# Weights asked for in nine pieces instead of six, and a new order of the steps: a linear-attention layer and a token and channel mixer on one core

## The chip, the cores and the metric

The kernel runs on one core of a Trainium2 chip. The time is the device time of one execution in microseconds; before the change its median is 165.49 us over 3 runs (165.25 to 165.77).

## What is computed

The inputs r, k and v have 4 batches, 8 heads, 768 positions and 48 values per head. A linear attention with decay `w` and bonus `u` runs along the positions; its output x has, for each batch, 768 positions of 384 values. Behind it stands a mixer: a two-layer net along the positions, added to x, and a two-layer net along the 384 channels, added again.

```python
def _attn_ref(r, k, v, w, u):
    for t in range(S):
        cur = np.einsum('bhd,bhe->bhde', u[None] * kt, vt)
        y[:, :, t] = np.einsum('bhd,bhde->bhe', rt, state + cur)
        state = w[None, :, :, None] * state + np.einsum('bhd,bhe->bhde', kt, vt)

def _moe_ref(x, w_tok1, w_tok2, w_ch1, w_ch2):
    xt = x.transpose(0, 2, 1)
    h = np.maximum(xt @ w_tok1, 0.0) @ w_tok2
    u = x + h.transpose(0, 2, 1)
    h2 = np.maximum(u @ w_ch1, 0.0) @ w_ch2
    return (u + h2)
```

## The kernel before

**The work.** The positions are cut into chunks of 128, six to a batch, so there are 24 units (a batch and a chunk), counted from 0. For each unit `u` the names of the steps are: `kp` and `rp`, the products of k and r with powers of the decay (tiles `kpr` from `ld_k` and `ld_r`), on VectorE or GpSimd; `vb`, a cast of v on ScalarE; `trk` and `trr`, their transposes on TensorE (`tr_ps`) and `rkk`, `rkr` or `rk`, the copies out of PSUM in two halves or in one (tile `rk`); `at`, the scores (`at_ps`); `AT0` and `AT1`, the masked scores, one half of which may go by ScalarE (`raw`); `kv` and `S`, the state; `pr` and `pg`, the bonus; `yd`, `yS` and `y`, the output (`y_ps`); `x`, the sum, which is the mixer's input (`x_b`).

For each batch `b` the mixer has: `hid`, the first token product over its six chunks (`h_ps<-x_b,wtok`), `hr`, its relu (`h1r`); then `bk` and `us`, the second token product and its sum by chunk (`hT_ps`, `u_sb`), and `tu` and `uT`, the turn of each chunk (`t_ps`, `uT`); in batch 0's first half `ux` and `ub` make it turned at once (`at_ps` and `ut_ps`). Then come the channel nets for each half batch: 12 up steps `z` (`z_ps<-uT,wch`) of three matmuls, each read by a relu `zr`, and for each of three chunks the down step `h` (`h_ps<-wch,zr`) in four quarters of three matmuls. Quarters 0 and 1 of a down step read the first half of `w_ch2`, quarters 2 and 3 the second. `os` adds and `out` stores. So `z0_0_4` is batch 0, half 0, up step 4, and `h0_1_2` batch 0, chunk 1, quarter 2.

**The order.** `Step` (L35) and `Plan` (L45) are a list scheduler that runs while the kernel is built: `graph` (L168) adds the steps with the engines that may do them, what they wait for and a rank; `Plan.run` (L72) puts them in an order of time with the durations that are written beside them; in this order every engine's instructions are issued, and each engine works strictly in that order. `Plan.fill` (L129) puts idle matmuls into gaps of TensorE ahead of the first up step. All instructions are recorded by one helper at L512, so the profile shows that line for nearly all.

**The weights.** The four mixer weights are read from float32 in memory to bf16 tiles by DMAs that GpSimd issues, between its products: `wtok1` and `wtok2` whole, `wch1` (the up weight) and `wch2` (the down weight) in halves. Their place in GpSimd's order comes from `wafter` in `CFG`. The loads of k, r and v are issued by SyncE in the order of `transfers`; unit 6's k, and so all behind it, waits for unit 5's output (`hold`).

Of the kernel before, what the change touches and what calls it, by code (L numbers as in the profile page):

```python
# [24 lines left out]
C = S // T  # L25
G = C // 2
HP = H // 2
NJ = 12
# [6 lines left out]
class Step:  # L35
    def __init__(self, name, ways, after, take, give, rank, emit):
# [3 lines left out]
        self.engine = self.start = self.end = self.seen = self.sends = None  # L40
        for a in self.after:
            a.then.append(self)


class Plan:  # L45
# [26 lines left out]
    def run(self):  # L72
# [5 lines left out]
        while todo:  # L78
# [4 lines left out]
            while again:  # L83
                again = False
                for s in sorted(open_, key=lambda s: (s.rank, s.ready)):
                    if s.ready > now or (s.take and min(banks) > now):
                        continue
# [6 lines left out]
                    way = min(s.ways, key=lambda w: max(now, free.get(w[0], 0.0)) + w[2] + (w[4] if len(w) > 4 else 0.0))  # L94
# [73 lines left out]
def graph(do, cfg):  # L168
# [25 lines left out]
    loads, weights, fetched, gates, u_row = {}, {}, [], {}, None  # L194
    for n, (kind, i) in enumerate(cfg["transfers"]):
# [3 lines left out]
        elif kind != "w":  # L199
# [5 lines left out]
        else:  # L205
            weights[i] = n
    wx, wi = {}, {}

    def weight(i, after):
        wi[i] = s = p.add(f"i:w{i}", [("POOL", 0.9, cfg.get("wseen", 1.0), True)], after, rank=-50, emit=do("weight", i))  # L210
        took = cfg.get("wtime", (3.0, 2.6, 3.1, 7.7, 3.1) if 5 not in cfg["wafter"] else (3.0, 2.6, 3.1, 3.9, 3.1, 3.9))[i]
        wx[i] = p.transfer(f"x:w{i}", s, took, took + 1.0, -1.0)

    for i in cfg["wafter"]:
        weight(i, [])
    xs, S_prev, at_free, y_free, kv_read, yS_prev = {}, None, [], None, None, None
    kv_first, bank_read, scored = None, [], {}
    for u in range(NU):
# [22 lines left out]
        else:  # L241
# [12 lines left out]
            if u in by_pe:  # L254
                pr = p.add(f"pr{u}", [("DVE", cfg.get("prt", 0.5), 0.65)], [rk], rank=r - 0.3, emit=do("pr", u))
                reads.append(pr)
# [65 lines left out]
    for b in range(B):  # L322
# [5 lines left out]
        bank = [p.add(f"hid{b}_bank{i}", [("PE", 0.0, 0.0)], early + [wx[0]], take=True, rank=r) for i in range(2)]  # L328
        for c in range(C):
            h = p.add(f"hid{b}_{c}", [("PE", 2 * MM * f, 2 * MM * f + 0.13)], [xs[b * C + c], h] + bank, rank=r, emit=do("hid", b, c))  # L330
# [12 lines left out]
        for sg in range(2):  # L343
            if (b, sg) in direct:
                last = C * (b + 1) - 1
                for mm in range(3):
# [4 lines left out]
                    t = p.add(f"ub{n}", [("PE", 2 * MM + 0.01, 2 * MM + 0.14)], [t, wx[1]] + (hr if mm else first), rank=r - 0.2 + 0.01 * mm, emit=do("ub", b, sg, mm))  # L351
# [5 lines left out]
            for c in range(sg * G, sg * G + G):  # L357
                n = 3 if (b, c) in cfg.get("xpe", ()) else 2
                bk = p.add(f"bk{b}_{c}", [("PE", n * MM + 0.01 * (b > 0), n * MM + 0.13 + 0.01 * (b > 0))], hr + [wx[1]], take=True, rank=r + 0.01 * c, emit=do("bk", b, c))
# [636 lines left out]
```

## Time and profile before

| What | Value |
|---|---|
| median of 3 runs | 165.49 us |
| span of the profiled execution, first to last instruction | 166.5 us |
| TensorE busy | 156.8 us, 94% |
| VectorE, ScalarE, GpSimd busy | 106.8, 87.2, 65.3 us |
| mean granted clock of TensorE | 0.990 |
| chain that ended last | TensorE 79%, DMA 8%, GpSimd 5%, ScalarE 3% |

The profiled execution is one run of its own; of its time only the span is shown, which is 1.0 us over the median of the runs. Times within the trace are microseconds from the start of the span. In a timeline row stand start, length, engine, line, instruction, tiles written and read, count, and in brackets the idle time ahead of it and what ended that. Rows of the same kind are merged. A busy TensorE is not one at its peak, so its busy time is read along with the granted clock.

### The profile page before, as it was taken

The numbers are of one execution on the slowest core, as the hardware profiler recorded it, in microseconds if no ns is written. First come the engines' busy times: TensorE is split into PE (matmuls) and PEld (weight loads), VectorE is DVE, ScalarE is ACT, GpSimd is POOL, SyncE is SP. The second block draws the span as 40 slices with busy tenths as digits, with TensorE's granted clock in tenths as the row PEclk, the third lists the DMA queues.
The fourth block names the chain that finished last, engine by engine and source line by source line (L and its number), as shares of the span: only waits on it lengthen the run. The fifth ranks groups of instructions, "written<-read, shape, count | busy, mean of one in ns | idle before, by whom it ended". The sixth has DMA issues, their size and how long they took to land.

```text
span 166.5 us, 3791 instructions
## 1 busy us (share of the span) xinstructions
PE 156.8 (94%) x1462; PEld 100.6 (60%) x1464; DVE 106.8 (64%) x219; ACT 87.2 (52%) x182; POOL 65.3 (39%) x80
## 2 busy tenths in 40 slices
PE   6797999599999999999999999999999999999991
PEld 1377764356677666666666665666656655665671
DVE  5189996300459989899989889977885582021031
ACT  3996743279198636579804452069154502904900
POOL 7839970000009647386785857103840000000000
PEclk9999999789999999999999999999999999999999
DMA  5999999999699899999999994999990028012012
GB/s 100 215 213 210 159 187 176 188 184 168 131 208 287 158 192 216 217 230 182 198 192 169 230 158 106 188 235 222 171 240 6 4 50 218 16 51 94 0 47 94
DMA packets 97427, 26.26 MB, mean 158 GB/s; under 512 B 90753, under 2 KB 97410, under 8 KB 97410
## 3 DMA queue, kind: packets, MB, share of 16 engines
q1 hardware_dynamic: 93920, 22.88, 67.2%
q0 software_dynamic: 3488, 3.15, 12.3%
q8 instruction: 11, 0.18, 0.5%
q14 instruction: 6, 0.05, 0.1%
q10 hardware_dynamic: 2, 0.00, 0.0%
HBM read 20.65 MB, written 4.72 MB: 152 GB/s over the span
## 4 chain that ended last, share of the span: by engine, by line
PE 79%; DMA 8%; POOL 5%; ACT 3%; issue 2%; DVE 1%; SPq 1%; POOLq 0%
PE h_ps L512 31%; PE z_ps L512 29%; DMA wch<-in_moe_w_ch_dram 6%; PE y_ps L512 4%; PE at_ps L512 4%; PE hT_ps L512 3%; PE tr_ps L512 3%; POOL kpr L512 3%; PE kv_ps L512 2%; DMA ld_v<-in_v_dram 2%; PE t_ps L512 1%; ACT rk L512 1%; POOL wtok L512 1%; SPq L512 1%; POOL yd L512 0%
## 5 line engine op out<-in xcount | busy, mean ns | idle before, releaser
L512 ACT ACTIVATE zr<-z_ps 128x384 bf16<-128x384 f32 x94 | 45.5, 492 | 47.5 <-PE z_ps L512 47.3
L512 PE MATMUL z_ps<-uT,wch 128*128 128x384 bf16 x288 | 53.6, 331 | 2.0 <-DMA wch<-in_moe_w_ch_dram 2.0
L512 PE MATMUL h_ps<-wch,zr 128*128 128x384 bf16 (+1 forms) x300 | 52.5, 319 | 0.0
L512 PEld LDWEIGHTS <-wch 128*128 128x128 bf16 x288 | 27.0, 99 | 18.8 <-DMA wch<-in_moe_w_ch_dram 2.4
L512 PEld LDWEIGHTS <-zr 128*128 128x128 bf16 x300 | 27.9, 98 | 15.5 <-issue 0.2
L512 POOL TENSOR_TENSOR yd<-vb,adg 128x384 f32<-128x384 bf16 x18 | 15.5, 860 | 46.5 <-ACT adg L512 27.9
L512 DVE TENSOR_TENSOR AT<-at_ps,mask 128x512 bf16<-128x512 f32 x43 | 27.9, 682 | 0.7 <-PE at_ps L512 0.6
L512 DVE TENSOR_TENSOR osb<-u_sb,h_ps 128x384 f32<-128x384 bf16 (+1 forms) x22 | 11.7, 533 | 23.4 <-PE h_ps L512 23.3
L512 POOL TENSOR_TENSOR kpr<-ld_r,wp 128x384 bf16<-128x384 f32 x16 | 16.6, 1036 | 5.3 <-ACT wp L512 2.8
L512 ACT COPY rk<-tr_ps 128x512 bf16<-128x512 bf16 (+1 forms) x20 | 15.0, 756 | 4.9 <-PE tr_ps L512 4.5
L512 PEld LDWEIGHTS <-kpr 128*128 128x128 bf16 x192 | 13.7, 107 | 6.0 <-POOL kpr L512 2.6
L512 DVE TENSOR_TENSOR x_b<-y_ps,yd 128x384 bf16<-128x384 f32 x24 | 13.2, 552 | 5.2 <-PE y_ps L512 5.1
L512 POOL TENSOR_TENSOR kpr<-ld_k,wn 128x384 bf16<-128x384 f32 x15 | 15.2, 1011 | 1.8 <-DMA ld_r<-in_r_dram 0.7
L512 PEld LDWEIGHTS <-rk 48*128 48x128 bf16 (+1 forms) x272 | 11.0, 99 | 6.4 <-issue 2.7
L512 ACT CAST vb<-ld_v 128x384 bf16<-128x384 f32 x24 | 12.3, 511 | 4.3 <-POOL kpr L512 3.1
L512 PE MATMUL tr_ps<-ident,kpr 128*128 128x128 bf16 x112 | 12.1, 245 | 2.4 <-ACT rk L512 1.4
L512 DVE TENSOR_TENSOR S<-kv_ps,bm 128x384 bf16<-128x384 f32 x13 | 7.2, 551 | 6.0 <-PE kv_ps L512 5.8
L512 DVE TENSOR_TENSOR u_sb<-x_b,hT_ps 128x384 bf16<-128x384 bf16 x21 | 10.4, 546 | 0.9 <-PE hT_ps L512 0.9
L512 PEld LDWEIGHTS <-wtok 128*128 128x128 bf16 x90 | 8.0, 98 | 4.8 <-issue 0.6
L512 PEld LDWEIGHTS <-AT 128*128 128x128 bf16 x192 | 8.4, 98 | 3.4 <-DVE AT L512 0.8
L512 PE MATMUL at_ps<-rk 48*128 48x128 bf16 x192 | 10.2, 229 | 0.2 <-ACT rk L512 0.2
L512 PE MATMUL h_ps<-x_b,wtok 128*128 128x384 bf16 x48 | 10.2, 326 | 0.0
(81 smaller groups left out, 145.4 us busy)
## 6 DMA issues: line engine op xcount, KB each, us to landing
ld_k<-in_k_dram SPq DMA_DIRECT2D x24, 192.0 KB, 3.8
ld_r<-in_r_dram SPq DMA_DIRECT2D x24, 192.0 KB, 3.8
ld_v<-in_v_dram SPq DMA_DIRECT2D x24, 192.0 KB, 3.8
out_dram<-osb SPq DMA_DIRECT2D x23, 192.0 KB, 2.6
wch<-in_moe_w_ch_dram POOLq DMA_DIRECT2D x4, 576.0 KB, 14.2
wtok<-in_moe_w_tok_dram POOLq DMA_DIRECT2D x2, 384.0 KB, 6.4
u_bc<-in_u_dram SPq DMA_DIRECT2D x1, 192.0 KB, 5.0
out_dram<-osb SPq DMA_DIRECT2D x2, 96.0 KB, 1.6
```

Of the source, the lines that this page charges most:

```text
L512: ins = tc.keep_in_program_order(f(*args, **kw))
```

## The change

The list `wafter` goes; `pieces` takes its place. Each row of it names a weight, a range of its chunks, a planned duration and the step behind which it may be issued. The token weights and the first half of `w_ch1` are now read in two pieces each (so the two pieces of that half are quarters of the up weight); the other half of `w_ch1` and the two of `w_ch2` stay as they were. Each step of the mixer waits only for the pieces that it reads. Ranks of single steps (`rank`) and pins of single steps to an engine (`on`) are added; the units whose half of the scores goes by ScalarE (`raw`) and whose copies are made in halves (`rk_two`) are other ones, and so are a few planned durations. The scheduler's loop is also written to run faster, with the same rules.

```diff
@@ graph
-        elif kind != "w":
+        else:
-    for i in cfg["wafter"]:
-        weight(i, [])
+    for i, (of, lo, hi, took, after) in enumerate(cfg["pieces"]):
+        wi[i] = s = p.add(f"i:w{i}", [("POOL", 0.85, cfg.get("wseen", 1.0), True)], rank=-50 + 0.01 * i, emit=do("weight", i))
+        wx[i] = p.transfer(f"x:w{i}", s, took, took + cfg.get("wland", 1.3), -1.0 + 0.001 * i)
+
+    def got(of, lo, hi):
+        return [wx[i] for i, (o, a, b, _, _) in enumerate(cfg["pieces"]) if o == of and a < hi and b > lo]
...
-                z = p.add(f"z{b}_{sg}_{j}", [("PE", 3 * MM, 3 * MM + 0.13)], old + uT[3 * sg:3 * sg + 3] + [wx[2] if j < NJ // 2 else wx[4]], take=True, rank=m + 0.1 * sg + 0.001 * j, emit=do("z", b, sg, j))
+                z = p.add(f"z{b}_{sg}_{j}", [("PE", 3 * MM, 3 * MM + 0.13)], old + uT[3 * sg:3 * sg + 3] + got("c1", j, j + 1), take=True, rank=m + 0.1 * sg + 0.001 * j, emit=do("z", b, sg, j))
...
-    for i, name in cfg["wafter"].items():
-        p.wait(wi[i], [last] + [next(s for s in p.steps if s.name == name)])
+    for i, piece in enumerate(cfg["pieces"]):
+        p.wait(wi[i], [last] + [next(s for s in p.steps if s.name == piece[4])])
...
+        if s.name in cfg.get("on", {}):
+            s.ways = [w for w in s.ways if w[0] == cfg["on"][s.name]]
+            s.open_on = s.ways[0][0] if len(s.ways) == 1 else None
@@ CFG
-    + [('w', 0), ('w', 1), ('w', 2), ('w', 4), ('w', 3), ('w', 5)],
-    wafter={0: 'x:r4', 1: 'x:r4', 2: 'rp5', 4: 'kp5', 3: 'rp5', 5: 'rp5'},
-    slack={'v5': 3.0},
+    pieces=[
+        ('t1', 0, 3, 1.45, 'x:k4'),
+        ('t1', 3, 6, 1.45, 'x:r4'),
+        ('t2', 0, 3, 1.25, 'x:k5'),
+        ('c1', 0, 3, 1.9, 'rp4'),
+        ('t2', 3, 6, 1.25, 'rp5'),
+        ('c1', 3, 6, 1.9, 'kp4'),
+        ('c1', 6, 12, 3.3, 'x:r5'),
+        ('c2', 0, 6, 4.0, 'rp4'),
+        ('c2', 6, 12, 4.0, 'x:r5')],
+    slack={'v5': 1.6},
-    raw=(0, 1, 5, 8, 11),
-    rk_two=(0, 1, 2, 3, 4, 6),
+    raw=(0, 1, 4, 5, 6, 10, 13, 18, 19),
+    rk_two=(0, 1, 2, 3, 5, 6, 7),
-    pe_times=((0.33, 0.243, 0.185), (0.33, 0.243, 0.185)),
+    pe_times=((0.42, 0.21, 0.175), (0.42, 0.21, 0.175)),
+    rank={
...
+        'yS14': -0.1295, 'yS16': 985.0098, 'yS21': -1.239, 'yd4': -0.5759, 'z0_0_10': -0.2839, 'z0_0_3': 0.0102,
+        'z0_0_4': -0.4424, 'z0_0_8': -0.4755, 'z0_1_10': -0.0249, 'z0_1_3': -0.3309, 'z0_1_8': -0.1011,
...
+    on={
+        'adg8': 'ACT', 'hr0_0b': 'DVE', 'hr2_0': 'ACT', 'hr3_0': 'DVE', 'kp0': 'DVE', 'kp15': 'POOL', 'kp17': 'DVE',
+        'kp19': 'POOL', 'kp21': 'DVE', 'kp4': 'DVE', 'kp7': 'POOL', 'kp9': 'POOL', 'ku19': 'DVE', 'ku20': 'POOL',
...
@@ weight
-        t, src = [(wtok1, moe_w_tok1), (wtok2, moe_w_tok2), (wch1, moe_w_ch1), (wch2, moe_w_ch2), (wch1, moe_w_ch1), (wch2, moe_w_ch2)][i]
+        of, lo, hi = CFG["pieces"][i][:3]
+        t, src = {"t1": (wtok1, moe_w_tok1), "t2": (wtok2, moe_w_tok2), "c1": (wch1, moe_w_ch1), "c2": (wch2, moe_w_ch2)}[of]
+        rows, cols = (slice(lo, hi), slice(None)) if of in ("t1", "c2") else (slice(None), slice(lo * 128, hi * 128))
```

The first place is GpSimd's order around the weight issues. Before, from unit 2's r product (`kpr_122`) on; `kpr_124` is unit 3, `kpr_126` unit 4 and the second `kpr_118` unit 5, `wtok` are the token weights and `wch_148` and `wch_149` the up and the down weight:

```order
L512 TENSOR_TENSOR kpr_122<-ld_r,wp 128x8x48
L512 TENSOR_TENSOR kpr_124<-ld_k,wn 128x8x48
L512 TENSOR_TENSOR kpr_124<-ld_r,wp 128x8x48
L512 TENSOR_TENSOR kpr_126<-ld_k,wn 128x8x48
L512 DMA wtok_146<-in_moe_w_tok_dram 128x6x256
L512 TENSOR_TENSOR kpr_126<-ld_r,wp 128x8x48
L512 DMA wtok_147<-in_moe_w_tok_dram 128x2x768
L512 TENSOR_TENSOR kpr_118<-ld_k,wn 128x8x48
L512 TENSOR_TENSOR kpr_118<-ld_r,wp 128x8x48
L512 DMA wch_148<-in_moe_w_ch_dram 128x3x768 x2
L512 DMA wch_149<-in_moe_w_ch_dram 128x6x384 x2
```

And now, at the same place on GpSimd:

```order
L554 TENSOR_TENSOR kpr_124<-ld_k,wn 128x8x48
L554 TENSOR_TENSOR kpr_122<-ld_r,wp 128x8x48
L554 DMA wtok_146<-in_moe_w_tok_dram 128x3x256
L554 TENSOR_TENSOR kpr_126<-ld_r,wp 128x8x48
L554 DMA wtok_146<-in_moe_w_tok_dram 128x3x256
L554 TENSOR_TENSOR kpr_118<-ld_k,wn 128x8x48
L554 DMA wtok_147<-in_moe_w_tok_dram 128x2x384
L554 TENSOR_TENSOR kpr_118<-ld_r,wp 128x8x48
L554 DMA wch_148<-in_moe_w_ch_dram 128x3x384
L554 DMA wtok_147<-in_moe_w_tok_dram 128x2x384
L554 DMA wch_148<-in_moe_w_ch_dram 128x3x384
L554 DMA wch_148<-in_moe_w_ch_dram 128x3x768
```

Unit 3's r product and unit 4's k product have left GpSimd (they are VectorE's now), the first token weight's first half has moved ahead of unit 4's r product, and a piece stands between unit 5's k and r products; behind unit 5's r product come five more and the two halves of the down weight.

The second place is TensorE at the end of batch 0's token mixing, from the last `bk` on. Before:

```order
L512 MATMUL hT_ps<-h1r,wtok_147 128x384
L512 LDWEIGHTS wch_148 [waits DVE_49,DMASW4_49]
L512 MATMUL z_ps<-uT,wch_148 128x384 [waits Activation_49]
...
L512 LDWEIGHTS u_sb [waits DVE_49]
L512 MATMUL t_ps<-ident,u_sb 128x128
```

And now (the number behind DMASW counts GpSimd's DMAs from 0 and starts over behind 7; two small ones for `w` and `u` are 0 and 1, so that weight piece n, counted from 1, is n + 1):

```order
L554 MATMUL hT_ps<-h1r,wtok_147 128x384
L554 LDWEIGHTS u_sb [waits DVE_49]
L554 MATMUL t_ps<-ident,u_sb 128x128
...
L554 LDWEIGHTS wch_148 [waits DMASW7_49]
L554 MATMUL z_ps<-uT,wch_148 128x384 [waits Activation_49]
...
L554 LDWEIGHTS wch_148 [waits DMASW5_49]
L554 MATMUL z_ps<-uT,wch_148 128x384 [waits Activation_49]
```

Before, the first up step followed the token mixing at once and three turns followed it; now two of the three turns (six matmuls) stand ahead of the first up step, which is `z0_0_4` and waits for the sixth piece; the last turn and `z0_0_0`, which waits for the fourth, follow.

The third place is TensorE where the second half of the down weight is first read: before it, at both times, stand quarters 0 and 1 of the first three down steps. Before, that was `z0_1_4` and then `h0_0_2`, which waits for the last piece:

```order
L512 LDWEIGHTS wch_148
L512 MATMUL z_ps<-uT,wch_148 128x384 [waits Activation_49]
...
L512 LDWEIGHTS zr
L512 MATMUL h_ps<-wch_149,zr 128x384 [waits DMASW7_49]
...
L512 LDWEIGHTS kpr_120 [waits DVE_49]
L512 MATMUL tr_ps<-ident,kpr_120 128x128 [waits Activation_49]
```

Now it is `z0_1_0` and then `h0_1_2`, with the last piece's number 2:

```order
L554 LDWEIGHTS wch_148
L554 MATMUL z_ps<-uT,wch_148 128x384 [waits Activation_49]
...
L554 LDWEIGHTS zr
L554 MATMUL h_ps<-wch_149,zr 128x384 [waits DMASW2_49]
...
L554 LDWEIGHTS kpr_120 [waits DVE_49]
L554 MATMUL tr_ps<-ident,kpr_120 128x128 [waits DVE_49]
```

Ahead of this place stood 17 up steps, and now 16. Behind it, in both orders, the transposes of unit 6's products (`kpr_120`) follow.

37 lines of the change are left out of this document (16 added, 21 removed), and 25 rows, old and new, of tables (on, rank).

## The prediction, made before the changed kernel ran

> **What bounds the kernel now.** I read the page's first lines, then the table of busy time by stretch (columns: stretch, its length, busy us and count of each engine, granted TensorE clock, DMA share, GB/s), with cuts at the first up step, the first down step and the last matmul.
>
> ```profile
> span 166.5 us, 3791 instructions
> ...
> PE 156.8 (94%) x1462; PEld 100.6 (60%) x1464; DVE 106.8 (64%) x219; ACT 87.2 (52%) x182; POOL 65.3 (39%) x80
> ```
> ```profile
> 0.00:30.90 30.90, 25.12 (x259) 16.37 (x261) 21.82 (x57) 19.16 (x40) 19.27 (x32) 1.00 1.02 181
> 30.90:41.10 10.20, 10.18 (x58) 6.15 (x59) 1.27 (x3) 7.75 (x16) 0.00 (x0) 0.83 1.19 185
> 41.10:163.20 122.10, 121.53 (x1147) 78.12 (x1144) 83.34 (x159) 60.27 (x127) 46.05 (x48) 1.00 0.73 152
> 163.20:166.50 3.30, 0.00 (x0) 0.00 (x0) 0.34 (x1) 0.00 (x0) 0.00 (x0) 1.00 0.19 61
> ```
>
> From 41.10 us TensorE is busy 121.53 of 122.10 us at the full clock: a new order there can win back 0.57 us and no more, and can only add waits. What can be won stands ahead of 41.1 us: idle time, and in the second stretch a mean clock of 0.83. Next the timeline of TensorE (start, length, instruction, in brackets idle time and what ended it) around the first up step.
>
> ```profile
> 27.76 1.14 PE L512 MATMUL hT_ps<-h1r,wtok 128*128 128x384 bf16 x6
> 30.92 0.85 PE L512 MATMUL z_ps<-uT,wch 128*128 128x384 bf16 x3 [2.02 <-DMA wch<-in_moe_w_ch_dram]
> 31.57 1.26 PE L512 MATMUL t_ps<-ident,u_sb 128*128 128x128 bf16 x9
> 32.62 8.49 PE L512 MATMUL z_ps<-uT,wch 128*128 128x384 bf16 x45
> ...
> 44.38 0.65 PE L512 MATMUL z_ps<-uT,wch 128*128 128x384 bf16 x3
> 44.86 1.14 PE L512 MATMUL h_ps<-wch,zr 128*128 128x384 bf16 x6
> ```
> ```profile
> 29.00:30.90 1.90, 0.00 (x0) 0.00 (x0) 0.90 (x2) 0.00 (x0) 0.00 (x0) 1.00 1.16 195
> 31.40:34.40 3.00, 3.00 (x17) 1.84 (x15) 0.72 (x2) 1.46 (x3) 0.00 (x0) 0.50 1.25 184
> 34.80:38.00 3.20, 3.20 (x21) 1.93 (x20) 0.56 (x1) 3.18 (x7) 0.00 (x0) 1.00 1.28 185
> ```
>
> Two losses stand side by side. TensorE has nothing to do for 2.02 us, because the first half of the up weight hasn't landed. Right behind that the granted clock is 0.50 for some 3.4 us: by the mean of 0.83 over 10.20 us, 0.17 x 10.20 = 1.73 us of full-clock work are missing. Together 3.75 us, the budget of this change. The DMA share is above 1.0 all through: what lands when is a matter of the order of bytes.
>
> **The change part by part.** *The products and the weight issues on GpSimd.* Its timeline before:
>
> ```profile
> 11.82 1.00 POOL L512 TENSOR_TENSOR kpr<-ld_r,wp 128x384 bf16<-128x384 f32 x1 [2.77 <-ACT wp L512]
> 12.78 1.00 POOL L512 TENSOR_TENSOR kpr<-ld_k,wn 128x384 bf16<-128x384 f32 x1
> 14.14 1.25 POOL L512 TENSOR_TENSOR kpr<-ld_r,wp 128x384 bf16<-128x384 f32 x1 [0.36 <-DVE AT L512]
> 15.35 0.99 POOL L512 TENSOR_TENSOR kpr<-ld_k,wn 128x384 bf16<-128x384 f32 x1
> 16.29 0.90 POOL L512 DMA_DIRECT2D wtok<-in_moe_w_tok_dram  x1
> 17.20 1.01 POOL L512 TENSOR_TENSOR kpr<-ld_r,wp 128x384 bf16<-128x384 f32 x1
> 18.15 0.78 POOL L512 DMA_DIRECT2D wtok<-in_moe_w_tok_dram  x1
> 18.95 1.01 POOL L512 TENSOR_TENSOR kpr<-ld_k,wn 128x384 bf16<-128x384 f32 x1
> 19.91 0.99 POOL L512 TENSOR_TENSOR kpr<-ld_r,wp 128x384 bf16<-128x384 f32 x1
> 20.86 3.26 POOL L512 DMA_DIRECT2D wch<-in_moe_w_ch_dram  x4
> ```
>
> rp3 and kp4 (14.14 and 15.35) go to VectorE, so the first weight piece is issued behind kp3 and rp2 alone: from 13.8 us at the earliest, I take 14.4, 1.9 us sooner than 16.29. In front of rp5 (19.91) stand now three issues, not two: 3.26 / 4 = 0.82 us more, against 2.0 us of products that left. So GpSimd is ready for rp5 sooner, and the landing of r5 decides. A load that is asked for just ahead of a weight lands late: the slowest v load took 6.9 us, the median 3.8.
>
> ```profile
> L512 SPq DMA_DIRECT2D ld_v<-in_v_dram x3: 902/1238/1707, 10.1 to 15.9; - x3
> ...
> DMA to landing us min/median/max: 3.8/3.8/6.9
> ```
>
> That is 3.1 us behind the whole first token weight, asked for 0.4 us after that load; behind half of it about 1.55. rp5 found r5 ready at 19.91, so r5 lands by then, in the new order some 20.7 at my estimate (bounds: 19.1, nothing in the way, and 22.3, both halves), and rp5 ends at 21.7 instead of 20.90. Of this the copies of unit 5 give back a part, as its second half is copied by itself:
>
> ```profile
> 19.07 0.59 ACT L512 COPY rk<-tr_ps 128x512 bf16<-128x512 bf16 x1
> ...
> 21.49 1.01 ACT L512 COPY rk<-tr_ps 128x1024 bf16<-128x1024 bf16 x1 [1.29 <-PE tr_ps L512]
> ```
>
> 1.01 - 0.59 = 0.42. So token mixing ends 0.8 - 0.4 = 0.4 later, at 29.3 instead of 28.90 (27.76 + 1.14). kp0, rp1, rp3 and kp4 on VectorE cost nothing beyond this: VectorE's last work ahead of the mixing, unit 5's output, is reached by way of rp5 all the same. If that cover is missing, each costs 0.55 us on VectorE (its product rows), 2.2 at most; I take 0.
>
> *More mixing ahead of the first up step.* Six of the nine turns now stand ahead of it. They ran from 31.57 to 32.62, nine in 1.05 us at about half the clock, so 0.058 each at the full one: 0.35 us go into the idle time. First up step ready: 29.3 + 0.35 = 29.65.
>
> *The pieces.* The quarters do less than their name: the order shows that the first up step waits for the sixth piece, the second quarter, and the next for the fourth, the first quarter. So the same bytes as before (token weights and half the up weight) have to be there.
>
> ```profile
> L512 POOL DMA_DIRECT2D wch<-in_moe_w_ch_dram x4: 775/818/861, 20.9 to 23.3; - x4
> ...
> DMA to landing us min/median/max: 10.0/14.2/19.0
> ```
>
> The first half landed at 20.86 + 10.0 = 30.9, the last piece of the down weight at 23.3 + 19.0 = 42.3. In the new order the second quarter is issued third behind rp5, at 21.7 + 2 x 0.82 = 23.3. Bounds for its landing: 29.0 (the whole stream 1.9 sooner) and 33.3 (10.0 after its issue). I take 30.3, near the 30.9 of equal bytes, as the stream starts sooner but is interrupted for rp5. The first up step starts at 30.3, **0.6 sooner**; TensorE's idle time shrinks from 2.02 to about 30.3 - 29.3 - 0.35 = 0.65 us, in two pieces.
>
> *The clock.* The list of TensorE's waits (total us, times, longest):
>
> ```profile
> PE z_ps L512 <- DMA wch<-in_moe_w_ch_dram: 2.0, 1, 2.0
> PE tr_ps L512 <- ACT rk L512: 1.4, 2, 0.9
> ```
>
> The idle time of 2.0 us came with a drop of the granted clock; one of 0.9, earlier, with none in the rows. With 0.65 I take no drop: **1.73 sooner**. Bounds: 0 and 1.73.
>
> *The last piece.* With all this TensorE comes early to the first step that needs the down weight's second half, 44.86 before. One up step fewer stands ahead of it now (0.48 us, from 44.38 to 44.86). So 44.86 - 0.48 - 0.6 - 1.73 - 0.35 = 41.7 us. The piece landed at 42.3; its bounds now are 40.4 (1.9 sooner) and 44.75 (three more issues of 0.82). I keep 42.3, where the bytes put it: a **wait of 0.6**.
>
> *The rest.* Ranks and pins reorder units 6 to 23 and put 38 of the 96 relu copies of the up steps on VectorE (2 before), which has 83 of 122 us in that stretch: no term, between 0.57 won and 1.5 lost to new waits. Sum: -0.6 - 1.73 - 0.35 + 0.6 = -2.1 us on the span, 164.4. The median of the three runs, 165.49, is 0.994 of the profiled span (nothing else of that execution's time is shown), so 164.4 x 0.994 = **163.4 us**.
>
> **The rivals.** *The clock drops all the same* (0.15). Then 1.73 stays lost, TensorE reaches the last piece at 43.4 and doesn't wait: -0.95, span 165.55, time 164.6. For it: the wait may come at 31 and not at 30.3, and two waits in a row make one idle stretch. The Trainium skill, "TensorE: Matmul & The Clock Gate", section "HAM oscillation — how this bites in real kernels", gives the rule "no PE-idle gaps >~3.4µs". By that rule the 2.02 us would not have brought the drop, something else would, and it would stay, so that the sum would be this rival's. The trace disagrees: 2.02 us idle, then 0.50.
>
> *The pieces lengthen the weight stream* (0.06). If each of the three added ones costs the stream one issue of 0.82, the last lands at 44.75, TensorE waits for it, and 44.75 - (44.86 - 0.48) = +0.4: span 166.9, time 165.9. Against it: between 31.4 and 38.0 the DMA share is 1.25 to 1.28 at 184 GB/s across the borders of pieces. The Trainium skill, "DMA: Bandwidth & Descriptors", section "Anatomy of one DMA — SWDGE (gpsimd) path", puts a fixed cost of about 2.0 us on each DMA. By that figure, paid in a row, the estimate would be 6 us more for the stream and a time near 169.4; the rows of unbroken DMA share speak against it.
>
> *Unit 5's r product comes late, and everything behind it* (0.22), the slower case. Price: both halves of the first token weight get in front of r5, 3.1 us; r5 lands at 22.3, rp5 ends at 23.3, 2.4 later; less 0.42, the mixing ends at 30.9. The pieces behind rp5 are issued 2.4 later too, the quarter at 24.9, so that it lands at about 32.3 (30.3 plus the 1.6 by which rp5 slips past my estimate, and 0.4 for work in between). TensorE idles over a microsecond again, the clock drops, and the up steps start 1.4 later than now; less 0.35: +1.05, span 167.6, time 166.5. It decides from about 22.5 us as rp5's end; the row of v at 6.9 us speaks for it, r5's place ahead of v5 in its queue against.
>
> **How the numbers follow.** The forecast has 0.57; it spans 161.6 (first up step at 29.65, no wait for the last piece, the 0.57 won back: -1.27 - 1.73 - 0.35 - 0.57 = -3.9, span 162.6) to 164.9 (1.5 lost later). The rivals reach 164.6, 165.9 and 166.5. The range 161.6 to 166.5 leaves out the upper half of the slow case and little below. A measurement of this kernel can tell about 0.3%, 0.5 us, from no change. Faster: 0.53 + 0.13; same: 0.04 + 0.02 + 0.03 + 0.02; slower: 0.03 + 0.20.
>
> **What would show it.** Right: the bracket before the first z_ps at 0.2 to 1.0 us and not 2.02; no stretch at 0.50 after 20 us; the first z_ps between 29.6 and 31; six t_ps ahead of it; a short wait of h_ps for wch near 42 us; busy time after that within 0.6 us of the stretch. Wrong: rp5 ending behind 22.5, a row of half clock at 31 to 35, or new TensorE waits of over 1 us among units 6 to 13, where products and loads are late by the new order.

## The result, and the profile after

The changed kernel is slower: 166.41 us (median of 6 runs, 165.85 to 167.12) beside 165.33 us (6 runs of before, 164.87 to 165.77); ratio 1.0076, interval 1.0048 to 1.0104. The forecast was 163.4 us. The profiled execution is the one of 167.12 us; its span is 165.4, and over all six runs the time is 1.7 to 1.8 us above the span (165.85 us has 164.1). The ratios here and below leave out the few executions that are over 1.5% above the fastest of their kernel, and they aren't the quotients of the medians beside them.

If that holds for the profile of before on which the prediction rests, with its span of 166.5, this was an execution of about 168.2 us, 2.7 us above the median and not an ordinary one; ordinary ones have spans near 163.8. I therefore profiled before again (run e1 below, span 164.0, 165.67 us) and compare with that. First the page's first lines of the changed kernel, then its table by stretch, cut at the first up step, 10.2 us behind it, and at the last matmul (columns as for before):

```profile
span 165.4 us, 3778 instructions
PE 156.1 (94%) x1461; PEld 100.7 (61%) x1462; DVE 122.0 (74%) x256; ACT 73.1 (44%) x151; POOL 66.2 (40%) x82
```
```profile
0.00:31.10 31.10, 26.27 (x265) 17.34 (x267) 23.82 (x61) 19.88 (x42) 17.71 (x31) 1.00 0.99 170
31.10:41.30 10.20, 10.20 (x72) 6.44 (x72) 2.79 (x6) 6.47 (x14) 0.00 (x0) 1.00 1.25 189
41.30:161.70 120.40, 119.47 (x1128) 76.90 (x1125) 95.06 (x189) 46.71 (x96) 48.52 (x51) 1.00 0.75 156
```

The same stretches, relative to the first up step, in e1:

```profile
0.00:29.65 29.65, 24.97 (x261) 16.09 (x261) 21.64 (x57) 19.04 (x40) 19.25 (x32) 1.00 1.01 179
29.65:39.85 10.20, 9.95 (x71) 6.28 (x72) 1.34 (x4) 8.17 (x17) 0.00 (x0) 1.00 1.25 192
39.85:160.40 120.55, 120.04 (x1136) 77.20 (x1133) 83.30 (x158) 59.57 (x125) 46.00 (x48) 1.00 0.73 155
```

In both the clock is 1.00 in the second stretch: the 0.83 of the first profile isn't there in the ordinary execution of before either. The first stretch is 1.45 us longer in the changed kernel, the rest about as long (130.60 and 130.75). So the loss lies ahead of the first up step. TensorE's timeline there in the changed kernel:

```profile
21.14 0.40 PE L554 MATMUL tr_ps<-ident,kpr 128*128 128x128 bf16 x4 [1.02 <-POOL kpr L554]
...
22.89 0.40 PE L554 MATMUL tr_ps<-ident,kpr 128*128 128x128 bf16 x4 [0.39 <-POOL kpr L554]
...
26.64 0.33 PE L554 MATMUL y_ps<-S,rk 128*128 128x96 bf16 x4 [0.48 <-DVE x_b L554]
...
30.17 0.49 PE L554 MATMUL hT_ps<-h1r,wtok 128*128 128x384 bf16 x2
30.49 0.64 PE L554 MATMUL t_ps<-ident,u_sb 128*128 128x128 bf16 x6
31.09 0.66 PE L554 MATMUL z_ps<-uT,wch 128*128 128x384 bf16 x3
```

The wait for `wch` is gone, the six turns stand ahead of the first up step, which starts without a bracket (though by little: the trace has the second quarter landed at 31.04, the step starts at 31.09); but mixing ends at 30.66 (30.17 + 0.49), and the two transposes of unit 5 (k, then r) wait for GpSimd. Its timeline:

```profile
14.38 0.81 POOL L554 DMA_DIRECT2D wtok<-in_moe_w_tok_dram  x1
15.95 1.24 POOL L554 TENSOR_TENSOR kpr<-ld_r,wp 128x384 bf16<-128x384 f32 x1 [0.76 <-DVE kpr L554]
17.13 0.82 POOL L554 DMA_DIRECT2D wtok<-in_moe_w_tok_dram  x1
20.11 0.98 POOL L554 TENSOR_TENSOR kpr<-ld_k,wn 128x384 bf16<-128x384 f32 x1 [2.15 <-DMA ld_k<-in_k_dram]
21.05 0.76 POOL L554 DMA_DIRECT2D wtok<-in_moe_w_tok_dram  x1
21.83 1.01 POOL L554 TENSOR_TENSOR kpr<-ld_r,wp 128x384 bf16<-128x384 f32 x1
```

Unit 5's k product waits 2.15 us for its load, and the r product behind it ends at 22.84, 1.79 later than in e1. The wait isn't all lateness, since GpSimd comes to the product sooner than in e1 (17.95, where the issue ends, against 19.09): the product starts 1.02 later, and the piece that now stands between the two products takes 0.76 more. Unit 5's r load, which the trace has landed at 21.41, would have held its product until about 21.55 without that piece (an estimate, with the 0.15 us that lie between the landing of k's load at 19.96 and its product). In e1 both run without a wait, and TensorE's lines show what before really loses there, 0.95 us:

```profile
19.09 1.01 POOL L512 TENSOR_TENSOR kpr<-ld_k,wn 128x384 bf16<-128x384 f32 x1
20.05 1.00 POOL L512 TENSOR_TENSOR kpr<-ld_r,wp 128x384 bf16<-128x384 f32 x1
```
```profile
27.56 1.14 PE L512 MATMUL hT_ps<-h1r,wtok 128*128 128x384 bf16 x6
29.66 0.66 PE L512 MATMUL z_ps<-uT,wch 128*128 128x384 bf16 x3 [0.95 <-DMA wch<-in_moe_w_ch_dram]
30.16 0.50 PE L512 MATMUL t_ps<-ident,u_sb 128*128 128x128 bf16 x6
```

### The profile page after: what moved, and what is told of

It is laid out like the page before. It is cut to its first block, busy times and chain, and to the rows that moved or that the text cites. A ratio compares the mean times of both kernels' runs of the same rounds, so it can differ in the third digit from the quotient of the medians.

```text
span 165.4 us, 3778 instructions
## 1 busy us (share of the span) xinstructions
PE 156.1 (94%) x1461; PEld 100.7 (61%) x1462; DVE 122.0 (74%) x256; ACT 73.1 (44%) x151; POOL 66.2 (40%) x82
## 4 chain that ended last, share of the span: by engine, by line
PE 74%; SPq 10%; DMA 7%; POOL 3%; issue 2%; ACT 1%; DVE 1%; POOLq 0%; ACTq 0%
PE h_ps L554 29%; PE z_ps L554 29%; SPq L554 10%; PE hT_ps L554 4%; DMA ld_v<-in_v_dram 4%; DMA ld_k<-in_k_dram 4%; PE y_ps L554 4%; PE at_ps L554 3%; POOL kpr L554 2%; PE kv_ps L554 2%; PE tr_ps L554 2%; PE t_ps L554 1%; ACT rk L554 1%; POOL yd L554 0%; PE fill_ps L554 0%
## 5 line engine op out<-in xcount | busy, mean ns | idle before, releaser
L554 PE MATMUL h_ps<-wch,zr 128*128 128x384 bf16 (+1 forms) x300 | 53.4, 320 | 0.0
L554 PE MATMUL z_ps<-uT,wch 128*128 128x384 bf16 x288 | 51.9, 326 | 0.0
L554 ACT ACTIVATE zr<-z_ps 128x384 bf16<-128x384 f32 x58 | 28.3, 491 | 48.3 <-PE z_ps L554 48.0
L554 DVE TENSOR_SCALAR zr<-z_ps 128x384 bf16<-128x384 f32 x38 | 20.3, 554 | 13.0 <-PE z_ps L554 12.3
L554 DVE TENSOR_TENSOR AT<-at_ps,mask 128x512 bf16<-128x512 f32 x39 | 25.8, 682 | 0.8 <-PE at_ps L554 0.6
L554 POOL TENSOR_TENSOR kpr<-ld_k,wn 128x384 bf16<-128x384 f32 x14 | 14.5, 1032 | 28.7 <-DVE zr L554 15.8
L554 POOL TENSOR_TENSOR yd<-vb,adg 128x384 f32<-128x384 bf16 x17 | 14.3, 839 | 16.2 <-DVE adg L554 7.0
L554 POOL TENSOR_TENSOR kpr<-ld_r,wp 128x384 bf16<-128x384 f32 x15 | 15.6, 1038 | 4.9 <-DVE kpr L554 2.2
L554 PE MATMUL h_ps<-x_b,wtok 128*128 128x384 bf16 x48 | 10.2, 326 | 0.0
```

The costliest lines, as they stand in the source:

```text
L554: ins = tc.keep_in_program_order(f(*args, **kw))
```

## Theory and rivals

**Theory.** The first weight piece, issued 2 us sooner (14.38 instead of 16.43 in e1), delays unit 5's loads; its k product is late, the mixing with it, and the first up step starts 1.4 us later. **Rivals:** nine pieces cost more than six by themselves; the new order (other ranks, more work on VectorE) is the slower one; the first up step, `z0_0_4`, waits for the second quarter.

Most of the experiments in one table (the text has the others), from the timelines of each profiled execution (us; the end of unit 5's r product on GpSimd, the start of its last `x_b` on VectorE, the end of mixing, the first up step, the start of the last matmul less that) and the ratio of the times to before, with its interval:

| run | r product | x_b | mixing | first z | to last | ratio |
|---|---|---|---|---|---|---|
| e1 before | 21.05 | 25.14 | 28.70 | 29.66 | 130.68 | 0.9999 (0.9969 to 1.0029) |
| changed | 22.84 | 27.21 | 30.66 | 31.09 | 130.54 | 1.0076 (1.0048 to 1.0104) |
| e8 changed | 21.99 | 26.37 | 29.82 | 30.84 | 130.75 | 1.0092 (1.0057 to 1.0127) |
| e2 | 21.28 | 26.02 | 29.47 | 29.79 | 130.23 | 1.0008 (0.9978 to 1.0038) |
| e3 | 23.24 | 27.50 | 31.06 | 30.89 | 130.35 | 1.0024 (0.9995 to 1.0054) |
| e4 | 22.48 | 26.53 | 30.09 | 29.93 | 130.52 | 1.0006 (0.9984 to 1.0028) |
| e12 | 20.86 | 26.86 | 30.31 | 30.62 | 129.90 | 1.0017 (0.9996 to 1.0038) |
| e7 | 20.78 | 26.15 | 30.33 | 30.64 | 129.81 | 0.9991 (0.9962 to 1.0021) |
| e13 | 21.89 | 26.28 | 29.73 | 30.04 | 130.30 | 1.0066 (1.0036 to 1.0096) |
| e10 | 21.30 | 26.11 | 29.67 | 29.50 | 130.35 | 0.9944 (0.9915 to 0.9974) |
| e17 | 20.71 | 26.41 | 29.97 | 29.81 | 130.35 | 0.9972 (0.9946 to 0.9997) |

A profile is one execution; the ratios carry the verdicts (a run's median is over 12 executions in the e rows, 6 in e8 and e15). The profiled ones aren't all ordinary: by their times, that of the changed kernel lies 0.71 us above its run's median and e3's 0.55, e13's lies 0.90 below and e6's 0.64. The ends of matmuls are modelled, so that in some rows the mixing ends up to 0.17 us behind the start of the first up step.

## The experiments

### Before and the changed kernel again: e1, e8

> The kernel before, unchanged, with a second profile. Theory (its first profiled execution was an unlucky one: after's executions last 1.7 us longer than their spans, so 165.3 us would be a span near 163.6 and not 166.5): the spans lie near 163.6, TensorE's wait ahead of the first up step is about 1 us, and the clock shows no stretch at 0.50; ratio 1.000. Rival (the wait of 2 us and the clock drop belong to every execution): spans near 166, a mean clock of 0.990 in each.

165.36 us; no drop of the clock, and a wait of 0.95 instead of 2.02 us (rows above). The rival that the first profile was typical falls.

> The changed kernel unchanged, as a control beside the others of this call. Theory: 166.2 to 166.6 us, ratio 1.005 to 1.010; unit 5's last product on GpSimd ends at 22.5 to 23, the first z_ps starts at 30.8 to 31.3. Rival (the first comparison was a matter of its runs): 165.3 to 165.9 us, ratio within 0.998 to 1.003.

166.84 us (166.16 to 168.01). The changed kernel is slower again. Here the r product ends at 21.99, mixing and turns by 30.3, and then the first up step waits:

```profile
19.25 0.99 POOL L554 TENSOR_TENSOR kpr<-ld_k,wn 128x384 bf16<-128x384 f32 x1 [1.65 <-PE g_ps L554]
```
```profile
30.84 0.66 PE L554 MATMUL z_ps<-uT,wch 128*128 128x384 bf16 x3 [0.54 <-DMA wch<-in_moe_w_ch_dram]
```

The k product's bracket names TensorE, but k's load landed at 19.11, 0.14 us ahead of the product's start, as in the first profile (19.96 and 20.11): it is the same wait. In this execution the second quarter is the last to come, as the third rival has it. Three of the six executions have a mean clock of 0.987 to 0.990, where the first six had 0.996 and more; the profiled one isn't among them, so where their clock dropped wasn't seen. With e13 below, the changed order with the early first piece has such a clock in 7 of 24 executions; the runs of it that issue that piece later (e2, e7, e12, e14, e16) in 1 of 60.

### The first piece alone: e2 and e3

```diff
 changed kernel, order on GpSimd
-wtok1 0:3 | rp4 | wtok1 3:6 | kp5
+rp4 | wtok1 0:3 | wtok1 3:6 | kp5
```

> After, with the first token piece issued behind unit 4's r product, right ahead of the second piece; nothing else changes. Theory (that piece's bytes get ahead of unit 5's k and make everything behind it late): k5's product no longer waits for its load, rp5 ends near 21.5 instead of 22.84, the first up step starts near 29.8 instead of 31.1, and the time falls by 1.0 to 1.4 us, to a ratio near 1.000 against the kernel before. Rival (the nine pieces or the new order further on cost it): the time stays within 0.4 us of after, ratio 1.005 to 1.010.

```profile
15.74 1.24 POOL L554 TENSOR_TENSOR kpr<-ld_r,wp 128x384 bf16<-128x384 f32 x1 [1.51 <-DVE kpr L554]
16.93 1.61 POOL L554 DMA_DIRECT2D wtok<-in_moe_w_tok_dram  x2
18.55 1.03 POOL L554 TENSOR_TENSOR kpr<-ld_k,wn 128x384 bf16<-128x384 f32 x1
```

No wait for `ld_k`, which landed at 18.33, 1.6 us sooner than in the changed kernel; 165.74 us, ratio 1.0008. One issue, moved by 2.5 us, takes back nearly the whole loss (from 1.0076 and 1.0092).

```diff
 before, order on GpSimd
-kp3 | rp3 | kp4 | wtok1 | rp4
+kp3 | wtok1 0:3 | rp3 | kp4 | wtok1 3:6 | rp4
```

> The kernel before, with only the first token weight cut in two and its first half issued 2.5 us sooner, behind unit 3's k product, at 13.8 us. Theory: k5 lands about 2 us later, rp5 ends 1 to 1.5 us later, and the kernel is slower by 0.8 to 1.4 us, ratio 1.005 to 1.008. Rival (pieces or later order): no difference, ratio 1.000 within 0.002.

```profile
13.89 0.81 POOL L512 DMA_DIRECT2D wtok<-in_moe_w_tok_dram  x1
...
21.02 0.98 POOL L512 TENSOR_TENSOR kpr<-ld_k,wn 128x384 bf16<-128x384 f32 x1 [1.85 <-DMA ld_k<-in_k_dram]
```

The same wait, 1.85 us, appears in the old order (`ld_k` landed at 20.85, in e1 at 18.75), and mixing ends 2.36 us later than in e1. The time rises only to 166.03 us, ratio 1.0024, less than expected and not told from 1: the first up step starts 1.23 us later, not 2.36, because the old kernel's own 0.95 us wait for the up weight stood there as a cover, and the turn's wait of 0.24 goes too.

### The pieces alone, the order alone: e4, e12

```diff
 before, what each issue of the old list asks for
-wtok1 | wtok2 | wch1 0:6 | wch1 6:12 | wch2 0:6 | wch2 6:12
+wtok1 0:3, 3:6 | wtok2 0:3, 3:6 | wch1 0:3, 3:6 | wch1 6:12 | wch2 0:6 | wch2 6:12
```

> The kernel before, its six weight issues cut into the same nine pieces as after, at their old places and in their old order. Theory (the early place costs, not the cutting): ratio within 0.003 of 1.000, the second quarter landing at most 0.8 us later than the half did. Rival (each added piece lengthens the stream by an issue of 0.82 us, or by more): the last piece lands 2.4 us later and the kernel is slower by 0.5 to 2 us, ratio 1.003 to 1.012.

165.57 us, ratio 1.0006: the nine pieces together cost nothing that is measured, though two more issues delay the r product by 1.4 us. That is a gain and a loss in one: e10 below cuts the up weight alone and has 0.9944, and the two intervals don't overlap. In this order the cut of the token weights costs about 0.6%.

```diff
 changed kernel, order on GpSimd
-wtok1 0:3 | rp4 | wtok1 3:6 | kp5 | wtok2 0:3 | rp5 | wch1 0:3 | wtok2 3:6 | wch1 3:6 | ...
+rp4 | wtok1 | wtok2 | kp5 | rp5 | wch1 0:6 | wch1 6:12 | wch2 0:6 | wch2 6:12
```

> The changed kernel's order with before's weights: six transfers, the two of the token weights between unit 4's last product and unit 5's first, the four of the channel weights behind unit 5's last. It keeps the other half of the change, as e4_before_nine_in_place kept the pieces. Theory (the new order is worth what its turns hide, and the places of the pieces are the whole loss): unit 5's last product ends at 20.6, mixing by 29.2, the first z_ps starts at 29.5 to 29.8 with its turns done; 164.9 to 165.4 us, ratio 0.997 to 1.000. Rival (the new order itself costs, by evictions moved from ACT to DVE): first z_ps at 29.7 but 166.0 us or more, ratio 1.004 or more.

165.76 us, ratio 1.0017, between both expectations and not told from 1. The r product is early, 20.86, as expected; mixing isn't, because its first matmuls wait for the whole `wtok1`:

```profile
23.02 0.82 PE L554 MATMUL h_ps<-x_b,wtok 128*128 128x384 bf16 x4 [0.77 <-DMA wtok<-in_moe_w_tok_dram]
```

So neither half of the change is measurably slow alone, and with e2 the loss is, nearly all of it, the place of the first piece.

### Which piece comes last: e7, e13, e14, e16

```diff
 e7, changed kernel, order on GpSimd
-wtok1 0:3 | rp4 | wtok1 3:6 | kp5 | wtok2 0:3 | rp5 | wch1 0:3
+rp4 | wtok1 0:3 | wtok1 3:6 | kp5 | rp5 | wtok2 0:3 | wch1 0:3
```

> The changed kernel with two edits: the first piece goes out right ahead of the second (behind unit 4's last product, as in the run e2_after_first_later), and the third piece right ahead of the fifth, so that no piece lies between unit 5's two products on GpSimd. Theory (what made the changed kernel slow is only how late unit 5's last product ends): it ends at 20.5 instead of 21.28 in e2_after_first_later and 22.84 in the changed kernel, the mixing ends by about 29.0, and the first z_ps starts at 29.0 to 29.5 unless its quarter is later: 165.0 to 165.4 us, ratio 0.998 to 1.000. Rival (by then another thing is the last, the evictions of the mixing or the quarter itself): first z_ps at 29.8 as in e2_after_first_later, 165.6 to 165.8 us, ratio 1.002.

165.32 us, ratio 0.9991. The time is as expected, the trace isn't: the r product ends at 20.78, but mixing now waits for the last token piece (`hT_ps`, 0.55 us), which stands behind a quarter of the up weight.

```diff
 e13, changed kernel, order on TensorE
-z0_0_4 | tu0_5 | z0_0_0 | z0_0_1 | z0_1_3 | z0_0_2
+z0_0_0 | tu0_5 | z0_0_1 | z0_0_2 | z0_0_4 | z0_1_3
```

> The changed kernel with one edit in its order: its first up step is z0_0_0, which needs only the first quarter of the up weight, and the two that need the second quarter (z0_0_4 and z0_1_3) stand behind z0_0_2. In the changed kernel the first up step is z0_0_4, so that the quarter that lands at 26.7 to 27.8 us is of no use and the one that lands at 30.8 to 31.0 is waited for. Theory (both the late mixing and the late second quarter hold the changed kernel; in e8_after_again the wait was 0.54 us): the first z_ps starts with the end of the turns, at 30.2 to 30.6; 0.3 us gained on the mean of executions, 166.2 to 166.4 us beside 166.6, ratio 1.005. Rival (the mixing alone holds it): first z_ps at 31.0, no gain, ratio 1.007 to 1.009. A third (the order was the whole loss): below 165.8 us, ratio 1.002 or less.

166.59 us, ratio 1.0066: no gain over the changed kernel that its interval shows. In the profile the first up step starts with the turns, 0.31 us behind the mixing, which holds it. Beside e8, whose r product and mixing end within 0.10 us of it, that is 0.80 us sooner, so that in an execution like e8's the second quarter costs this on top. The medians don't show it: four of the twelve executions have a clock of 0.986 to 0.990, and the profiled one is the second fastest of the twelve. What the second quarter costs in the median stays open.

```diff
 e14: the edits of e7 and e13 together
```

> The edits of e7_after_token_pieces_later and of e13_after_first_quarter_first together. Theory (what the changed kernel can give once no piece makes unit 5 late and its first quarter is used first): mixing and turns end at 29.8 to 30.3 and the first z_ps with them; 164.9 to 165.2 us, ratio 0.996 to 0.998. Rival (the new order's mixing is itself the later one by 0.5 us, by its wait for the DVE eviction x_b, and that is all that is left): 165.3 to 165.6 us as in e7_after_token_pieces_later, ratio 0.999 to 1.001.

165.80 us, ratio 1.0015 (0.9988 to 1.0041): the rival's number, by another cause. The r product ends at 20.31, and mixing waits even longer for the last token piece:

```profile
28.65 0.82 PE L554 MATMUL hT_ps<-h1r,wtok 128*128 128x384 bf16 x4 [0.94 <-DMA wtok<-in_moe_w_tok_dram]
```

```diff
 e16, changed kernel with e13's order on TensorE; on GpSimd
-wtok1 0:3 | rp4 | wtok1 3:6 | kp5 | wtok2 0:3 | rp5 | wch1 0:3 | wtok2 3:6 | wch1 3:6
+kp4 (from VectorE) | rp4 | wtok1 0:3 | wtok1 3:6 | kp5 | wtok2 0:3 | rp5 | wtok2 3:6 | wch1 0:3 | wch1 3:6
```

> The changed kernel with four edits: the first piece right ahead of the second (unit 5's loads in time), the last token piece ahead of the first quarter of the up weight (in e14_after_later_first_quarter_first mixing waited 0.94 us for it), the first quarter used first, and unit 4's k product back on GpSimd, where it fits into a wait of 1.5 us (in e2_after_first_later GpSimd waits there for VectorE). Theory (VectorE is busy without a gap up to the mixing in the changed order, so that a product of 0.55 us put on it makes the mixing 0.5 us later; that and the pieces are the whole loss): mixing ends at 28.8 to 29.3, the first z_ps starts at 29.3 to 29.8; 164.7 to 165.1 us, ratio 0.995 to 0.998. Rival (VectorE isn't what holds the new order): as e14_after_later_first_quarter_first without its wait, first z_ps at 29.8 to 30.4, 165.3 to 165.8 us, ratio 0.999 to 1.002.

166.04 us, ratio 1.0039 (1.0010 to 1.0069): a miss for both. The first up step starts at 29.75 as the theory had it, but the up weight's second half is then the piece that is late, for a later up step:

```profile
34.18 0.99 PE L554 MATMUL z_ps<-uT,wch 128*128 128x384 bf16 x5 [0.68 <-DMA wch<-in_moe_w_ch_dram]
```

In three of these four orders TensorE then waits for another piece; in e13 the mixing holds it.

### The up weight in quarters alone, and a product on VectorE: e10, e5, e6, e17

```diff
 e10, before, behind rp5
-wch1 0:6 | wch1 6:12 | wch2 0:6 | wch2 6:12
+wch1 0:3 | wch1 3:6 | wch1 6:12 | wch2 0:6 | wch2 6:12
```

> Before with one edit: the first half of the up weight asked for as two quarters; no other order. In e5_before_quarters_turns the first quarter was there at 26.7 and mixing ended at 29.3, but three waits of 0.3 us for evictions in the turns put ahead kept the first z_ps until 30.5. Theory (the wait for the half is all that before loses there): the first z_ps starts with the end of mixing, at 28.8 to 29.3, without a wait; 164.6 to 165.0 us, ratio 0.995 to 0.998. Rival (the three up matmuls that the first quarter allows only bring the same eviction waits behind them, in the turns): first z_ps at 28.8 to 29.3, then 0.6 to 0.9 us of waits for DVE in t_ps within the next 2 us; 165.2 to 165.5 us, ratio 0.999 to 1.001.

```profile
28.53 1.14 PE L512 MATMUL hT_ps<-h1r,wtok 128*128 128x384 bf16 x6
29.50 0.65 PE L512 MATMUL z_ps<-uT,wch 128*128 128x384 bf16 x3
29.99 1.08 PE L512 MATMUL t_ps<-ident,u_sb 128*128 128x128 bf16 x9
```

164.83 us (164.11 to 165.23), ratio 0.9944 (0.9915 to 0.9974): the wait for the half is gone, as the theory has it, and the kernel is faster than both by one edit. Time from issue to landing of the up and down weight's pieces, in e1 and in e10 (least, median, most):

```profile
DMA to landing us min/median/max: 8.6/12.8/17.6
```
```profile
DMA to landing us min/median/max: 5.4/9.0/15.4
```

The first piece lands 8.6 us behind its issue at 20.99 in e1 and 5.4 behind 21.25 in e10, at 26.65: nearly 3 us ahead of its use by `z0_0_0`, which stands first in before's order and needs no other piece of the up weight. The second quarter landed at 28.24 by the trace, also ahead of that: in this execution the two quarters came sooner than the one half of e1, at 29.61.

```diff
 e6, before, order on TensorE (e5: and e10's quarters, and z0_1_0 to z0_1_3 ahead of z0_0_6)
-z0_0_0 | tu0_3 | tu0_4 | tu0_5 | z0_0_1
+tu0_3 | tu0_4 | tu0_5 | z0_0_0 | z0_0_1
```

> Before with one edit: the six turn matmuls of chunks 3 to 5 stand ahead of the first up matmul. Theory: they fill 0.35 us of the 0.95 us in which TensorE waits for the half of the up weight; the first z_ps still starts at 29.6 to 29.7, what follows has 0.35 us less: 165.0 us, ratio 0.998. Rival (they delay the first up step by the evictions that they wait for, which end later than the half lands): first z_ps at 30.2 or later, 165.5 us or more, ratio 1.001 or more.

> Before's order with three edits: the first half of the up weight asked for as two quarters, the turn matmuls of chunks 3 to 5 ahead of the first up matmul, and four up matmuls of the second group ahead of the first group's seventh. Theory (the time is the start of the first up step plus about 130.5 us of packed TensorE work and 5.3 us behind it; in the ordinary execution of before 0.95 us of the start are a wait for the half): the first quarter is there by about 28.4, token mixing and turns end at about 29.05, no wait in the bracket of the first z_ps, which starts at 29.05 and has 0.35 us of turns less behind it: 0.95 us gone, 164.4 us beside 165.4, ratio 0.994. Rival (the wait only moves: the fourth z_ps waits for the second quarter, which lands as late as the half did plus a fixed price of a DMA, or the work behind is late next): first z_ps at 29.1 but 165.2 to 165.6 us, ratio 0.999 to 1.001.

e6: 165.67 us, 1.0011 (0.9992 to 1.0030); e5: 165.25 us, 0.9989 (0.9970 to 1.0008). Both theories miss. TensorE in e6:

```profile
28.84 1.27 PE L512 MATMUL t_ps<-ident,u_sb 128*128 128x128 bf16 x9
29.94 3.74 PE L512 MATMUL z_ps<-uT,wch 128*128 128x384 bf16 x22
```

Nine matmuls of the turns stand for 1.10 us ahead of the first up step; in e1 they take 0.90 behind `z0_0_0` (30.16 to 31.06, a wait of 0.24 in it), and at 0.058 us each, as the prediction has it, they would be 0.52. The first up step is 0.28 later than in e1, and in e5 it starts at 30.51. That the turns wait for VectorE's `u_sb` when they are put ahead, which the work behind `z0_0_0` hid before, fits this but wasn't tested alone.

```diff
 e17: e10 with unit 4's k product on VectorE; on GpSimd
-kp4 | wtok1 | rp4 | wtok2 | kp5 | rp5
+rp4 | wtok1 | wtok2 | kp5 | rp5
```

> e10_before_quarters with unit 4's k product on VectorE, as in the changed kernel, and unit 4's r product ahead of the first weight issue, so that this issue stays where it was, at 16.6 us. It sets the cost of the product on VectorE against the GpSimd time that it frees. Theory (VectorE is packed up to the mixing): unit 5's r product ends 1 us sooner, at 20.3, and still the last x_b is 0.5 us later, the first z_ps at 29.6 to 30.1 beside 29.1 to 29.5; 165.2 to 165.4 us, ratio 0.997 to 0.9985. Rival (unit 5's r product on GpSimd is what the mixing waits for): first z_ps 0.4 us sooner or more, 164.2 to 164.6 us, ratio 0.990 to 0.9935.

165.01 us, ratio 0.9972. The rival's ratio lies outside the interval: 0.6 us less on GpSimd gains nothing. But the intervals of e10 and e17 overlap, and the theory's mechanism isn't what the trace shows: VectorE has a gap, because unit 5's v is late for ScalarE, whose masked scores (`raw`) come behind it.

```profile
24.39 0.51 ACT L512 CAST vb<-ld_v 128x384 bf16<-128x384 f32 x1 [1.43 <-DMA ld_v<-in_v_dram]
```
```profile
25.41 0.42 DVE L512 TENSOR_TENSOR AT<-raw,mask_b 128x512 bf16<-128x512 bf16 x1 [0.62 <-ACT raw L512]
```

### The clock: e9, e11, e15

```diff
 before, the up weight's pieces (e9, e11, e15)
-wch1 0:6 | wch1 6:12
+wch1 0:8 | wch1 8:12
+wch1 6:8 | wch1 0:6 | wch1 8:12
+wch1 6:12 | wch1 0:6
```

> Before with the up weight asked for as eight chunks and four instead of six and six: the first up step then waits for a transfer a third longer. It is to tell what a longer wait there costs, and if the drop of the granted clock to 0.50 that stood behind the 2.02 us wait in the first profile comes with the length of the wait. Theory (the drop comes with about 2 us of idle TensorE in one stretch): the half-lands 1.3 us later, the bracket of the first z_ps is about 2.1 to 2.3 us, a stretch at 0.50 of some 3.4 us follows, and the time is 1.2 plus 1.7 us longer: about 168.2 us, ratio 1.017. Rival (the drop was the chip's, not the wait's): the bracket is the same, no stretch below 0.95 behind it, and the time is 1.2 us longer: 166.6 us, ratio 1.007.

> Before with the up weight asked for in another order: chunks 6 and 7 first, then 0 to 5, then 8 to 11. The first half comes about 1.3 us later by that (four chunks less than the 3.4 us between the two halves in e1_before_again, a third of them), so that TensorE waits about 2.2 us ahead of the first up step, which e9_before_eight_four failed to bring about (its wait was 0.66 us). Theory (the drop of the granted clock in the first profile came with the 2 us wait): in half of the executions or more a stretch at 0.50 of 3.4 us follows, these show a mean clock of 0.99 or below and a span 3 us above that of e1_before_again (167), the others one 1.3 us above it (165.3); median 167 to 168.4 us, ratio 1.010 to 1.018. Rival (the drop has another cause): the wait is there, the mean clock of every execution is 0.995 or more, 166.7 us, ratio 1.008.

> Before with the up weight's second half asked for ahead of its first, so that TensorE waits for a transfer that lands second. It is to bring about the long wait that e9_before_eight_four and e11_before_two_chunks_first did not (0.66 and 0.80 us). Theory (the drop of the granted clock in the first profile came with a wait of some 2 us): the half lands at 31 to 33, the bracket is 2.2 to 3.8 us, and a stretch at 0.50 of 3.4 us follows in most executions, their mean clock 0.99 or less; the time is 2 plus 1.7 us longer: 168.5 to 170 us, ratio 1.019 to 1.028. Rival (the drop has another cause): the wait is there, mean clock 0.995 or more, 167 to 168 us, ratio 1.010 to 1.016.

e9 and e11 don't bring the long wait: 0.66 us (first up step at 30.09, 166.16 us, 1.0039, 1.0007 to 1.0071) and 0.80 us (29.91, 165.63 us, 1.0016, 0.9994 to 1.0038), so they say nothing of the clock. e15 does: 169.19 us, ratio 1.0191 (1.0133 to 1.0249). Its wait, and two stretches behind it:

```profile
31.63 0.66 PE L512 MATMUL z_ps<-uT,wch 128*128 128x384 bf16 x3 [2.30 <-DMA wch<-in_moe_w_ch_dram]
```
```profile
32.20:35.20 3.00, 3.00 (x17) 1.85 (x16) 0.72 (x2) 1.46 (x3) 0.00 (x0) 0.50 1.27 184
35.80:39.00 3.20, 3.20 (x22) 1.96 (x20) 0.56 (x1) 2.99 (x7) 0.00 (x0) 1.00 1.27 193
```

Half clock for 3.4 us, from 0.55 us behind the end of 2.30 us of idle TensorE; in the first profile it came 0.34 us behind 2.02. Five of its six executions have a mean clock of 0.980 to 0.990. The one at 1.0 took 167.38 us, the least and still 2.0 us above before, so a longer start without the drop occurs too; its wait wasn't profiled. The theory holds for most executions, as it was put: the long wait brings the drop. The Trainium skill's rule "no PE-idle gaps >~3.4µs" ("TensorE: Matmul & The Clock Gate", section "HAM oscillation — how this bites in real kernels") is too generous for this case: 2.30 us was enough, 0.95 us in e1 was not.

## Why the prediction was wrong

- **The budget, the step that failed first.** "Together 3.75 us, the budget of this change" was read from one execution that was 2.7 us above the median. In the ordinary one the wait is 0.95 us and the clock stays at 1.00 (e1). So -1.73 had nothing to come from, and -0.6 turns round: the first up step forecast for 30.3 is 0.64 later than e1's 29.66. The two were more than the whole sum of -2.1. The mechanism behind 1.73 is real (e15), but before seldom meets it: of e1's twelve executions none has a mean clock below 0.996, and of the 145 others of before that stand beside the runs four have 0.99 or less.
- **"0.994 of the profiled span"** hid this. Time is span plus 1.66 to 1.79 us in every execution listed. A span of 166.5 under a median of 165.49 said that the profile was not of the median.
- **"rp5 ends at 21.7"** failed: 22.84, and 21.99 in e8. I asked how late r5 would land behind the early first piece, and never about k5, which is loaded ahead of it: its product waits 2.15 us. And r5 itself landed at 21.41, not 20.7, inside the bounds but later than taken. e3 (piece early in the old order, same wait) shows the cause of the wait, and e2 (piece later, loss gone) that it is nearly the whole loss. This is the rival "unit 5's r product comes late". Its 166.5 us is near the measured 166.41, but by errors that cancel: it started from the span that was too long, and counted on a clock drop that the profiled execution doesn't have.
- **The second quarter at 30.3** was 0.5 and 0.7 us too early: it landed at 30.79 in e8 and 31.04. Its issue slipped by 0.2 and 1.0 us (23.46 and 24.31 for 23.3), so the slip alone doesn't tell the landing. A quarter that is used first gains in the old order (e10); in the changed order the mixing is late all the same (e13).
- **The turns, -0.35:** the six run without a wait in the changed kernel, as predicted. In the old order they take 1.10 us there, not 0.35 to 0.52 (e6), which I hadn't looked at.
- **"kp0, rp1, rp3 and kp4 on VectorE cost nothing"** stays open. From the r product's end to `x_b` pass 4.37 us in the changed kernel and 4.09 in e1, but in the old order alone this goes from 4.05 (e4) to 4.81 (e10), so the difference tells nothing; e16 and e17 didn't settle it.
- **The last piece:** no wait at the predicted place; the piece landed at 42.06, near the 42.3 taken, and TensorE gets there at 42.49, not 41.7, since it started late. **The rest** of the order neither won nor lost: 130.54 us to the last matmul, 130.68 in e1. **The rival of a longer weight stream** falls: the last piece landed at 42.06, not 44.75, and in e4, with nine pieces at the old places, 0.76 us later than in e1 (41.76, 41.00), not 2.46.
- **Three small readings** that change no verdict: the two products that left GpSimd are 2.24 us by their rows, not 2.0; the DMA share is above 1.0 up to 41.1 us only (0.73 behind); and behind unit 5's r product stand four pieces and the two halves of the down weight, not five.

In e1's terms: mixing ends 1.96 us later, of which the old kernel's wait of 0.95 would have hidden a part; the turns between take 0.43; the first up step is 1.43 later, and the span 1.4. The medians differ by only 1.08: the profiled execution of the changed kernel is the slowest of its six. In how many executions of the changed kernel a clock drop adds to this, and where, stays open.

## What to carry to other kernels

Ahead of any sum, check that the profiled execution is an ordinary one: its own time, by the constant that lies between span and time, against the median; if it isn't, the largest waits in it are the least to be trusted. Where a transfer moves ahead, look at every load that is asked for around it, not only at the one that was last before, and at what its products feed. And separate the edits: quarters of one weight alone gave -0.56%, and this cut together with that of the token weights, an early first piece and a new order gave +0.76%.

## What the runs showed of the hardware that was not expected

- When a piece of weight lands isn't a matter of its bytes alone here. Eight chunks in place of six started the up steps only 0.43 us later than in e1 (30.09, 29.66), two chunks put ahead of the six only 0.25 later (29.91), and three chunks alone were there 3 us sooner (26.65). I had estimated 1.3 us for both of the first two. One execution each is little to go by: the same six chunks, issued at 20.86 and 20.99, landed at 30.88 in the first profile and at 29.61 in e1.
- A DMA of 192 KB issued on GpSimd's queue 2.5 us sooner made a load of 192 KB on SyncE's queue land later, by 1.6 us in the changed order (19.96 against 18.33 in e2) and by 2.1 in the old one (20.85 in e3, 18.75 in e1). In the changed order its issue, at 14.38, stood behind that load's own, at 14.11.
- The granted clock went to 0.50 for 3.4 us behind 2.02 and 2.30 us of idle TensorE, and not behind 0.95 us.
